# Cosine and sine rows of the inverse feature transform on two 64-row lanes of TensorE, with a new order

## Chip, cores and metric

One core of one Trainium2 chip runs the whole kernel. The time is device microseconds of one execution; the median of the runs counts. Engines are named as in the profile: PE (TensorE matmul) and PEld (its weight loads), DVE (VectorE), ACT (ScalarE), POOL (GpSimd) and SP (the queue that issues most DMAs).

## What is computed

Two mixers of the same x (2048 rows, 640 features) are blended row by row with a gate.

```python
def _A_ref(x, wqkv, wo):            # 32 heads of 20, 8 keys back at a distance of 2
    qkv = (x @ wqkv) ...
    logits = jnp.einsum("bhsd,bhswd->bhsw", q, kg) * scale
    attn = _softmax(jnp.where(mask, logits, -1e9), axis=-1)
    o = jnp.einsum("bhsw,bhswd->bhsd", attn, vg)
    return o.reshape(B, S, D) @ wo
def _B_ref(x, w_r, w_i):            # spectral filter
    X = jnp.fft.rfft2(x, axes=(-2, -1)) * (w_r + 1j * w_i)
    return jnp.fft.irfft2(X, s=(S, D), axes=(-2, -1))
g = _sigmoid((x * gate_w).sum(-1, keepdims=True))
return g * _A_ref(x, wqkv, wo) + (1 - g) * _B_ref(x, w_r, w_i)
```

## The kernel before

The 2048 rows are 16 p + j, with p on the 128 partitions and j = 0 to 15. `qkv` multiplies x with the projection (fp32 split into two fp32r parts, three products each) and stores the result to DRAM. `attend(par, h)` does four heads for the even or the odd j: DVE multiplies and reduces, POOL does the products with v (tiles pv), ACT copies, masks and the exponential. Its results (tiles o) go to DRAM (`od`) in pieces of two or four j, and `project_even`/`project_odd` read them back (`ot`), transpose them on PE (`oTp`) and multiply with wo (`woa`, `wob`).

The spectral branch folds x and transforms it over blocks of rows (`cols`, into `zg`), then sixteen groups g of frequencies run through `freq(g)`: the transform over features (u, v, ab), the rest of the row transform (x, z), the filter (P, wp), the two combinations s = P + z and P - z, and matmuls (tile `g`) that put rows of frequencies of the features onto the partitions of `zg`. Group 0 is the exception: two tables `back` instead of one, of which only some chunks of 128 need both.

`spatial(j)` is the inverse transform over features. Per j, six fp32 matmuls read `zg[:, t, j]` (t = 0 to 4, 128 feature frequencies each) as weights and `gt` (cosine and sine tables) as moving data, into two PSUM banks: `oa` gets the cosine rows and `ob` the sine rows, for even frequencies in the first 161 columns and odd ones in the next 161. The 128-row chunks straddle the four blocks of frequencies, so three of the chunks (1, 2 and 3) carry parts of two blocks, with zeros beside them. ACT copies both banks into `os`; four matmuls with `fct` (`ha`, `hb`) do the last step over rows, and ACT and DVE combine these with the attention's part into the output.

`work` records the operations in a natural order; `ORDER`, a table of numbers, then says in which order they are issued, and each engine runs its own in that order. All operations are issued through one line of the recorder (L386 before, L400 after), so tiles and not lines tell them apart. Each fp32 matmul shows as two MATMUL records in the trace. Buffers are rings of named places: `osr` (places for os), `ps(banks, name)` (PSUM banks). While the last heads of the attention are at work on DVE and POOL, PE runs `spatial` and the even projections; the odd projections are last, since they need the last heads.

Of the kernel before, what the change touches and what calls it, by code (L numbers as in the profile page):

```python
# [26 lines left out]

BP = (0, 1, 2, 3, 4, 5, 6)
# [3 lines left out]
def dft_tables():  # L32
# [7 lines left out]
    ke, ko = PERM[:161], PERM[161:]  # L40
    kb = PERM[2:161]
# [86 lines left out]
    def ck(k):  # L128
        return (np.where((k == 0) | (k == 320), 1.0, 2.0) / (S * D))[:, None]

    gt = np.zeros((640, 644))
    gt[0:161, 0:161] = np.cos(tau * np.outer(ke, d) / D) * ck(ke)
    gt[161:321, 161:322] = np.cos(tau * np.outer(ko, d) / D) * ck(ko) * (d < 160)
    gt[321:480, 322:483] = -np.sin(tau * np.outer(kb, d) / D) * ck(kb) * ((d > 0) & (d < 160))
    gt[480:640, 483:644] = -np.sin(tau * np.outer(ko, d) / D) * ck(ko) * (d > 0)
    gt = np.concatenate(
        [gt[0:128, 0:161], gt[128:256, 0:322], gt[256:384, 161:483], gt[384:512, 322:644], gt[512:640, 483:644]], 1
    )
# [15 lines left out]
class Engine:  # L154
# [50 lines left out]
{Wp48S^xk5{}S0j0stWa8~^|S5YJf5;2e()-dz9y0sAKZbW)=m>G~>ja#c?We=xxAfB@%${{m#x=b59`IdyTU{vq(yT@9sNe+BS{#HY+m)y=f!_RR8qRRBGA*}EW<uG2O+6A~}&R!D}&rV+x2jv1iJ  # L205
<-;gAir31;1Wf;>N>_o7_jkA<(T8Z}8f9+iVn*m~XGw&Dh4Q!g^!a-g;gRa_JDi6k#N9Iq<cZ2&JtcN76xX8*H9m++$L@A2#7kr>_z#tF%`KR?`)4zIcgHuNs+E`A0h0RujinI`1a|acnWK|Ere?@m
HR<GJdrLg8yDWOSIr*!MnId|XGp+qg;T23}HTJ=%(|W2(cSJH>)~(8ZXW6h>)0cUw(=(QERf0KOldi#P1i?WzT;Se6a||?lQgj~UmUG5v9Vn$>Bc}N8Iu)~M<1Wb(flHSj=Mu8b)c65D0UPTFIc$Q0
(eX9!O&5nj_$BX_(~F9Vbf!8Ozo0}fas_15zX7wEL;UuN2DXv*gTgLLBUH$^XgrP86i()d5+t3$VQRVU&`?%f)J^gaQkrt4YRK(uDSz6ys_<TP+v5B;kH9QqeHgo&uN?m5AydT{pLVlVOz{PO#Ijb6
+O)yXvOe&%NTw*a$ST7*T<`qoAH_gB75y1xXe|0>)lG%X*=7)4y&BU8^%*Xm6kh^Sg@lD{shw^{Z>fEm_IWhUF=K})%fC!6Fu70lFWo4rl)ap!;kHt`wJM?oKvv5;@mVMtBuwKD*4XhlYDu64#9kT{
LoY#86kzka)pPYf{N*4lfK|Z`J#<q`QZ_NaBFw(H%5Gx%$;!^X72{O@^sJrZv7k2nT2?{L0+;ot9F2h=*pz$=f&9oS(6R^=ve{df4Gv?SdS^LyH{tD9&i%;LlvR{wM*}SdvKKhASw?r!2at5#wz1@l  # L210
9qY$vBtM<%u&tdpjfO8Q;LOjzBL@R(X;g~)IPHm!_!rfJWL2THq&fzt!SDG>NLd6jG8dsdP1x#@MTG1W8uupzQlqVf<?Zn~FIA5l;+ETlX)e1Gvzk5Y(@KkltoII>Oq!}M<Uj%<$xl-i02$*HCS++k
zm7E!#<`$Z7Yt8Gk2*^Z@BvF>GQYM8Z*-TV?Kv0@qJF7f##CZ{y(YlGre6%8HrPr~ixycNU8D>G-?9=}{k$zQ7)`hKh3T2u(N}Khye~H#4Zu%~nt-$nP)gB+g_bvw;6!_2OJ1ZwNXWd+nivju$$Yw@
{h9EDLO`#cu0#7Fl%mr0w&ZwEG%_6<h{D)%uq5*G?j(=S$tlo1;dHxkC&sxr)AOMS7V~kRCl%$unp=pl>QB*_Gkdbs20DC$hI>tUiHYX@CRY0MrbuB|+IvRMnL`gm{`hUMh%=gs^!hX4hbW9<5mmSS
XEZ~;h~u_dmXo?8Ks6l!JlFu20k?{6q8m94^*#as=7R1ctF`$$B^`Ail-%HNAtoEC6QKtbyka-BLg;E<!xU!~^($8uvMN@^Y6q(}W%9@W9-)~@TzYtEg+@=5Z(Armx<=7lYZ?!>1G0&GS`i<jmKyP$
HmAy)ivl`kmitYwTKoN!Zj7@-A9p~Dpa((OWe??q%4t9K)exM$udFC_`SXg83|Ght1}1^%!o<snP@qnI*)XkJmJZ$d&YCSfYQ4?xSj$-`Xj5|lAR5Cuj9bI7u?u_BJd9=ihe<!VQVHaV^|bX~r-)1P
V|6MIih|dFGNQ4M`jqCg>Zn`!UA*cd)B3p;hV+tVJ3rxZOy2XSUYfTXSuav(Q*5M5P#?>UbaW1ZRvv_k#dt>44!0Qsa`V_FAqZ%H^GIWd<`o{JgMj3{Wx+e7*dmOf$J_K*J5{bxl(gOepgchq0O`!T
# [40 lines left out]
class Mixer:  # L257
# [17 lines left out]
    def places(self, pp, dr, sb):  # L275
# [15 lines left out]
        def ring(*tags):  # L291
            return Ring(sb, *tags)
# [24 lines left out]
    def ps(self, banks, name):  # L317
        if banks not in self.banks:
            self.banks[banks] = Ring(self.pp, *(f"bank{i}" for i in banks))
# [648 lines left out]
```

## Time and profile before

| what | value |
|---|---|
| median of 3 runs | 448.94 us (448.38 to 449.37) |
| profiled execution | 449.34 us, its span 447.5 us |
| PE busy | 438.6 us, 98% of the span |
| DVE busy | 408.7 us, 91% |
| POOL busy | 362.4 us, 81% |
| ACT busy | 211.2 us, 47% |
| DMA | 110.75 MB, 247 GB/s |

Groups of instructions are given as: engine, operation, out<-in by the program's names without numbers, shape, count, then busy time, mean duration of one in ns, and the engine's idle time before them with its cause. Chain rows give start, length and what ran; an "x8" counts records. In windows each engine's busy time stands in the order PE, PEld, DVE, ACT, POOL, followed by the granted clock of PE and the share and rate of DMA.

### The profile page before, as it was taken

Reading aid. Unit: us, or ns where it says so; the run is one execution under the profiler, and the core shown is the slowest. Engines: PE = TensorE matmul, PEld = TensorE weight load, DVE = VectorE, ACT = ScalarE, POOL = GpSimd, SP = SyncE. Lnnn points to the kernel's source line nnn. Section 1 sums busy time; section 2 is a strip of 40 time slices with the busy share of each in tenths; the row PEclk is TensorE's granted clock in tenths of the full one; section 3 lists DMA queues with packets and bytes.
Section 4 is the critical chain, followed back from the end, with each engine's and each line's share of the span. In section 5 each row is a group of like instructions: output and inputs, shape, how many; then the busy total and the mean of one; then the engine's idle time right before and its main releaser. Section 6 shows DMA issues by size and latency. Waiting matters only on the chain.

```text
span 447.5 us, 7258 instructions
## 1 busy us (share of the span) xinstructions
PE 438.6 (98%) x2440; PEld 390.1 (87%) x2440; DVE 408.7 (91%) x519; ACT 211.2 (47%) x561; POOL 362.4 (81%) x316
## 2 busy tenths in 40 slices
PE   9999999999999999999998999999999999999996
PEld 6888888888889889898887779998978999999996
DVE  4989989999999999999999999999999997899575
ACT  5443155363344634245548666677554564352110
POOL 1237984999999999997998999858899998899900
PEclk9999999999999999999999999999999999999999
DMA  8999999879489969789979789979976131366642
GB/s 325 390 349 321 313 325 369 299 205 312 131 240 325 341 181 325 204 279 313 319 219 311 235 274 297 313 218 308 295 200 204 31 99 42 96 218 228 184 177 88
DMA packets 73957, 110.75 MB, mean 247 GB/s; under 512 B 21297, under 2 KB 50993, under 8 KB 73921
## 3 DMA queue, kind: packets, MB, share of 16 engines
q1 hardware_dynamic: 40192, 69.32, 47.7%
q10 hardware_dynamic: 32816, 36.97, 26.7%
q0 software_dynamic: 912, 4.00, 2.3%
q8 instruction: 19, 0.31, 0.3%
q14 instruction: 18, 0.14, 0.1%
HBM read 72.51 MB, written 32.84 MB: 235 GB/s over the span
## 4 chain that ended last, share of the span: by engine, by line
PE 92%; DMA 2%; DVE 1%; ACT 1%; POOL 1%; issue 1%; ACTq 0%; POOLq 0%; DVEq 0%
PE qkv L386 47%; PE woa L386 8%; PE wob L386 7%; PE z L386 5%; PE ob L386 4%; PE oa L386 4%; PE g L386 4%; PE u L386 3%; PE v L386 2%; PE oTp L386 2%; PE ha L386 2%; PE x L386 2%; PE hb L386 2%; DMA P<-X 1%; DMA ot<-od 1%
## 5 line engine op out<-in xcount | busy, mean ns | idle before, releaser
L386 PE MATMUL qkv<-w,xo 128*128 128x480 f32 (+1 forms) x480 | 117.2, 388 | 0.0
L386 PE MATMUL qkv<-w,xe 128*128 128x480 f32 (+1 forms) x474 | 106.8, 382 | 0.0
L386 PEld LDWEIGHTS qkv<-w,xe 128*128 128x128 f32 x474 | 89.5, 189 | 14.8 <-ACT w L386 0.5
L386 PEld LDWEIGHTS qkv<-w,xo 128*128 128x128 f32 x480 | 88.4, 189 | 12.2
L386 ACT COPY ev<-qkv 128x480 f32<-128x480 f32 x64 | 35.1, 560 | 60.5 <-PE qkv L386 50.3
L386 PE MATMUL woa<-wo,oT 128*128 128x320 f32 x240 | 51.3, 330 | 0.2 <-DVE oT L386 0.2
L386 PE MATMUL wob<-wo,oT 128*128 128x320 f32 x240 | 49.5, 323 | 0.0
L386 POOL TENSOR_TENSOR P<-P,wp 128x963 f32<-128x963 f32 (+1 forms) x16 | 35.4, 2210 | 7.3 <-DMA P<-X 7.3
L386 PEld LDWEIGHTS woa<-wo,oT 128*128 128x128 f32 x240 | 38.2, 189 | 1.4 <-DVE oT L386 0.6
L386 PEld LDWEIGHTS wob<-wo,oT 128*128 128x128 f32 x240 | 37.7, 189 | 0.5 <-ACT ya L386 0.2
L386 POOL TENSOR_TENSOR fx<-fx 128x158 f32<-128x158 f32 (+1 forms) x16 | 11.7, 748 | 25.0 <-DVE fx L386 18.5
L386 POOL TENSOR_TENSOR w<-raw,w 128x480 fp32r<-128x480 f32 (+1 forms) x20 | 25.2, 1275 | 6.6 <-ACT w L386 6.5
L386 ACT CAST oT<-oTp 128x384 fp32r<-128x384 f32 (+1 forms) x32 | 13.2, 427 | 33.7 <-PE wob L386 13.2
L386 PEld LDWEIGHTS g<-mm,s 128*128 128x128 f32 x150 | 21.7, 190 | 6.0 <-ACT zg L386 4.0
L386 PE MATMUL g<-mm,s 128*128 128x128 f32 x150 | 24.9, 281 | 1.5 <-ACT zg L386 1.5
L386 PE MATMUL ob<-gt,zg 128*128 128x161 f32 (+1 forms) x96 | 22.7, 345 | 0.0
L386 PE MATMUL oa<-gt,zg 128*128 128x161 f32 (+1 forms) x96 | 22.6, 345 | 0.0
L386 PE MATMUL v<-bt,zc 128*128 128x240 f32 (+2 forms) x96 | 21.2, 327 | 1.1 <-ACT zc L386 1.1
L386 PE MATMUL u<-bt,zc 128*128 128x240 f32 (+2 forms) x96 | 20.8, 323 | 0.4 <-DVE ab L386 0.4
L386 DVE TENSOR_TENSOR oT<-oTp,oT 128x384 fp32r<-128x384 f32 (+1 forms) x32 | 15.1, 484 | 4.8 <-ACT oT L386 4.4
L386 PEld LDWEIGHTS v<-bt,zc 128*128 128x128 f32 x96 | 16.0, 190 | 4.0 <-ACT zc L386 1.4
L386 ACT CAST w<-raw 128x480 fp32r<-128x480 f32 (+1 forms) x30 | 17.0, 593 | 4.9 <-DMA raw<-in_wqkv 2.1
(304 smaller groups left out, 1120.0 us busy)
## 6 DMA issues: line engine op xcount, KB each, us to landing
qkvd<-ev ACTq DMA_DIRECT2D x32, 480.0 KB, 5.3
wp<-in_ws SPq DMA_DIRECT2D x16, 642.0 KB, 5.4
raw<-in_wqkv SPq DMA_DIRECT2D x25, 240.0 KB, 5.9
fx<-in_x SPq DMA_DIRECT2D x8, 641.0 KB, 7.5
ot<-od SPq DMA_DIRECT2D x16, 320.0 KB, 4.2
P<-X ACTq DMA_DIRECT2D x30, 160.5 KB, 4.7
fd<-fx POOLq DMA_DIRECT2D x6, 640.0 KB, 5.9
f<-fd SPq DMA_DIRECT2D x6, 640.0 KB, 5.6
```

The costliest lines, as they stand in the source:

```text
L386: p.dve.memset(w, 0.0)
```

## The change

`gt` is laid out anew. Frequencies 1 to 320 of the features go in five strips of 64, and a strip's cosine rows lie on partitions 0 to 63 (lane 0), its sine rows on partitions 64 to 127 (lane 1). `freq` writes s in that form: strip t has 64 sums and 64 differences side by side as one 128-column weight. The sine of frequency 320 is zero, and its place in lane 1 takes the constant term, which is therefore the first column of `ob` and is added to the even cosine part as the bias of an ACTIVATE. In `spatial`, ten matmuls of 64 rows take the place of six of 128: for each strip one from lane 0 into `oa` and one from lane 1 into `ob`, recorded as one operation by the new `Engine.run`, so that nothing comes between them. The program gives lane 0 the upper half of the array (position 0, size 64x128) and lane 1 the lower half (position 64).

Group 0 now uses both tables for all five strips (ten matmuls instead of six). ACT's two copies to `os` become three operations, and one ACTIVATE of one column for each group writes the constant term. `oa` and `ob` take turns through four banks instead of three, `ha` has bank 4 alone for odd j and banks 4 and 7 for even j, and `os` has five places instead of three. The tables that follow from this are smaller (`gt` 968 columns for 1288).

```diff
+STRIPS = (
+    (2, (0, 322), (0, 323)),
+    (0, (0, 161), (0, 162)),
+    (1, (0, 161), (1, 161)),
+    (3, (161, 161), (162, 161)),
+    (4, (161, 161), (162, 161)),
+)
...
+    gt, c = np.zeros((128, 968)), 0
+    for t, *parts in STRIPS:
+        for lane, (a, n) in enumerate(parts):
+            gt[64 * lane : 64 * lane + 64, c : c + n] = lanes[lane, 64 * t : 64 * t + 64, a : a + n]
+        c += n
...
+    def run(self, name, parts):
+
+        def all_of(parts):
+            for a, k in parts:
+                getattr(self.real, name)(*a, **k)
+
+        self.plan.record(self.eng, "run", all_of, (parts,), {})
...
 ORDER = """
-{Wp48S^xk5{}S0j0stWa8~^|S5YJf5;2e()-dz9y0sAKZbW)=m>G~>ja#c?We=xxAfB@%${{m#x=b59`IdyTU{vq(yT@9sNe+BS{#HY+m)y=f!_RR8qRRBGA*}EW<uG2O+6A~}&R!D}&rV+x2jv1iJ
+{Wp48S^xk5{}S0j0stWa8~^|S5YJf5;2b*)YFz*T0sAKZbW)=m>G~>ja#c?We=xxAfB@%${{m#x=b59`IdyTU{vq(yT@9sNe+BS{#HY+m)y=f!_RR8qRRBGA*}EW<uG2O+6A~}&R!D}&rV+x2jv1iJ
...
-        self.osr, self.hor, self.hyr, self.yer = n("raw", 3), n("x", 4), ring("x4", "x5"), ring("x6")
+        self.osr, self.hor, self.hyr, self.yer = ring("raw0", "raw1", "raw2", "ev0", "ev1"), n("x", 4), ring("x4", "x5"), ring("x6")
...
-        s = self.s12r.next(f"s{g}", 768)
-        d0 = 321
+        s = self.s12r.next(f"s{g}", 10 if g == 0 else 5, 2, 64)
+        sums = s[:, 0:5, 0], s[:, 5:10, 1] if g == 0 else s[:, :, 1]
+        pz = [a.rearrange("p (t r) -> p t r", t=5) for a in (P[:, 0, 1:321], z[:, 1:321])]
+        V.tensor_add(sums[0], *pz)
+        V.tensor_sub(sums[1], *pz)
         if g == 0:
-            d0 = 449
-            G.memset(s[:, 384:449], 0.0)
-        V.tensor_add(s[:, 0:321], P[:, 0], z)
-        V.tensor_sub(s[:, d0 : d0 + 319], P[:, 0, 2:], z[:, 2:])
+            G.memset(s[:, 0:5, 1], 0.0)
+            G.memset(s[:, 5:10, 0], 0.0)
+            G.memset(s[:, 5, 1, 0:1], 0.0)
+        A.activation(out=s[:, 0, 1, 0:1], in_=z[:, 0:1], func=AF.Identity, bias=P[:, 0, 0:1])
...
-                for w, back in chunks[t0 + i]:
+                for back in range(2 if g == 0 else 1):
...
-        o1, o2 = (self.ps((0, 1, 2), f"o{i}{j}") for i in "ab")
-
-        def mm(o, t, r, start, stop):
-            T.matmul(o, zg[:, t, j], r, start=start, stop=stop, skip_group_check=True)
-
-        mm(o1[:, 0:322], 1, gt[:, 161:483], True, False)
-        mm(o1[:, 0:161], 0, gt[:, 0:161], False, False)
-        mm(o1[:, 161:322], 2, gt[:, 483:644], False, True)
-        mm(o2[:, 0:322], 3, gt[:, 805:1127], True, False)
-        mm(o2[:, 0:161], 2, gt[:, 644:805], False, False)
-        mm(o2[:, 161:322], 4, gt[:, 1127:1288], False, True)
-        os = self.osr.next(f"os{j}", 644)
-        oq = os.rearrange("p (b a d) -> p a b d", b=2, a=2)
-        A.copy(oq[:, 0], o1[:, 0:322].rearrange("p (b d) -> p b d", b=2))
-        A.copy(oq[:, 1], o2[:, 0:322].rearrange("p (b d) -> p b d", b=2))
+        o1, o2 = (self.ps((0, 1, 2, 3), f"o{i}{j}") for i in "ab")
+        parts, c = [], 0
+        for t, *halves in STRIPS:
+            for i, (o, (a, n)) in enumerate(zip((o1, o2), halves)):
+                part = o[:, a : a + n], zg[64 * i : 64 * i + 64, t, j], gt[64 * i : 64 * i + 64, c : c + n]
+                parts.append((part, dict(start=(t == 2), stop=(t == 4), skip_group_check=True)))
+            c += n
+        T.run("matmul", parts)
+        os = self.osr.next(f"os{j}", 645)
+        A.copy(os[:, 322:645], o2[:, 0:323])
+        A.activation(out=os[:, 0:161], in_=o1[:, 0:161], func=AF.Identity, bias=os[:, 322:323])
+        A.copy(os[:, 161:322], o1[:, 161:322])
         yield
-        h1, h2 = self.ps((3, 4), f"ha{j}"), self.ps((5,), f"hb{j}")
+        h1, h2 = self.ps((4,) if j % 2 else (4, 7), f"ha{j}"), self.ps((5,), f"hb{j}")
```

The order changes from its 382nd operation on. On PE, at the first `oa` of the kernel, the six matmuls of an index stood among those of its neighbours and among `hb` and the transposes (the number behind a name is j, or the group for g; the number after the underscore is the buffer's):

```order
L386 MATMUL oTp0_860<-ident_69,ot12_858 128x128 x3
L386 MATMUL g15_3_815<-mm13_771,s15_813 128x128 x2
L386 MATMUL oa3_878<-gt_327,zg_211 128x322
L386 MATMUL oa1_872<-gt_327,zg_211 128x322
L386 MATMUL oa1_872<-gt_327,zg_211 128x161 x2
L386 MATMUL ob1_873<-gt_327,zg_211 128x322
L386 MATMUL ob1_873<-gt_327,zg_211 128x161
L386 MATMUL oa3_878<-gt_327,zg_211 128x161
L386 MATMUL ob1_873<-gt_327,zg_211 128x161
L386 MATMUL ob3_879<-gt_327,zg_211 128x322
L386 MATMUL hb1_876<-os1_874,fct_71 128x161
```

Now the same place on PE begins a stretch of lanes alone (L177 is the line in `Engine.run`):

```order
L400 MATMUL g15_3_815<-mm13_771,s15_813 128x128 x2
L400 MATMUL oTp0_860<-ident_69,ot12_858 128x128 x3
L177 MATMUL oa1_872<-gt_327,zg_211 128x322
L177 MATMUL ob1_873<-gt_327,zg_211 128x323
L177 MATMUL oa1_872<-gt_327,zg_211 128x161
L177 MATMUL ob1_873<-gt_327,zg_211 128x162
L177 MATMUL oa1_872<-gt_327,zg_211 128x161
L177 MATMUL ob1_873<-gt_327,zg_211 128x161
```

Lanes 0 and 1 alternate, and four indices (1, 3, 5, 7) follow one another, 40 matmuls, before PE comes to `oTp`, `ha` and `hb` again. In all the 160 matmuls on lanes stand in five such stretches, of 40, 30, 50, 30 and 10.

On ACT, just behind the same place, the banks were emptied in this order (vt4a is a load that ACT issues, qbank, L5b and ya belong to the attention):

```order
L386 COPY qbank_63<-q4b_576 128x160
L386 COPY os1_874<-oa1_872 128x2x161
L386 DMA vt4a_565<-qkvd_64 128x1200
L386 COPY os1_874<-ob1_873 128x2x161
L386 COPY os3_880<-oa3_878 128x2x161
L386 COPY qbank_63<-q4b_576 128x160
L386 ACTIVATE ho1_877<-hb1_876,ng_74 128x322
L386 COPY os3_880<-ob3_879 128x2x161
L386 COPY os5_885<-oa5_883 128x2x161
```

And now, for j = 3, 5 and 7 (L4a is a mask that ACT writes into the logits of the head, after DVE has made them):

```order
L400 COPY os3_880<-ob3_879 128x323
L400 ACTIVATE os3_880<-oa3_878,os3_880 128x161
L400 COPY os5_885<-ob5_884 128x323
L400 COPY os7_891<-ob7_890 128x323
L400 DMA q4b_576<-qkvd_64 128x640
L400 COPY L4a_567<-low_80 1x16x4
L400 ACTIVATE os5_885<-oa5_883,os5_885 128x161
L400 COPY os5_885<-oa5_883 128x161
L400 ACTIVATE L5b_551<-L5b_551 128x256
L400 ACTIVATE os7_891<-oa7_889,os7_891 128x161
L400 COPY os7_891<-oa7_889 128x161
```

The `oa` of j = 5 is emptied behind the mask L4a, and that of j = 7 behind L5b's exponential.

On DVE, around the last reduce of the attention (o4b6, for j = 13 and 15), the order was:

```order
L386 TENSOR_REDUCE o4a6_596<-pv4a6_597 128x160
L386 TENSOR_TENSOR y12_974<-ha12_967,h12_969 128x321
L386 SCALAR_TENSOR_TENSOR y1_981<-woa1_992,g_73,y1_981 128x320
L386 TENSOR_TENSOR oT5_997<-oTp0_998,oT5_997 128x384
L386 TENSOR_TENSOR oT5_997<-oTp3_999,oT5_997 128x256
L386 TENSOR_REDUCE o4b6_598<-pv4b6_599 128x160
L386 SCALAR_TENSOR_TENSOR y1_981<-wob1_993,g_73,y1_981 128x320
```

And it is now:

```order
L400 SCALAR_TENSOR_TENSOR y1_981<-wob1_993,g_73,y1_981 128x320
L400 SCALAR_TENSOR_TENSOR ha14_975<-ha14_975,ng_74,h14_977 128x161
L400 TENSOR_TENSOR y14_979<-ha14_975,h14_977 128x321
L400 TENSOR_TENSOR oT5_997<-oTp3_999,oT5_997 128x256
L400 TENSOR_REDUCE o4a6_596<-pv4a6_597 128x160
L400 SCALAR_TENSOR_TENSOR y3_987<-woa3_1000,g_73,y3_987 128x320
L400 TENSOR_TENSOR oT7_1005<-oTp0_1006,oT7_1005 128x384
L400 TENSOR_TENSOR oT7_1005<-oTp3_1007,oT7_1005 128x256
L400 TENSOR_REDUCE o4b6_598<-pv4b6_599 128x160
```

The reduce comes behind the outputs of j = 1 and the combination of j = 14, ahead of which it stood: 477th of DVE's 519 instructions, where it was 474th.

More of the change, by code (lines that the diff above doesn't have):

```diff
@@ L129, in ck @@
         return (np.where((k == 0) | (k == 320), 1.0, 2.0) / (S * D))[:, None]
[L131 to L138, printed above, removed]
+    lanes = np.zeros((2, 320, 323))
+    for at, a, k, fits in ((0, 0, PERM[1:161], (d > 0) & (d < 160)), (160, 161, ko, d > 0)):
+        fitc = (d < 160) | (at == 0)
+        lanes[0, at : at + 160, a : a + 161] = np.cos(tau * np.outer(k, d) / D) * ck(k) * fitc
+        lanes[1, at : at + 160, a + 1 : a + 162] = -np.sin(tau * np.outer(k, d) / D) * ck(k) * fits
+    lanes[1, 0] = 0
+    lanes[1, 0, 0] = 1 / (S * D)
+    gt, c = np.zeros((128, 968)), 0
[3 more added lines that the diff above has]
+        c += n
     f = np.float32
@@ new lines @@
+FIo&uC=rTCG^332n*e4@1I8_Pp|;?Q1QFGcxB-#|GS~LA(^EhN(DVpb`MU*=byh=F*yquh`Iq5#d?5nVCXAf*aAFNz{Y_VOzYE1HXf2WN=7dJ8-xDM>9wt;XARM*?l4cr!x?wJ$fC;lQ#AlkYSvttQ
+LM14tn$Xj8dih9p`Md<VH3fwii9;yN3D{BfoQ2BOOCobu3f?3aoqk01r})J1v31zZR6FVz01KW(1seb{62BuarlL@`TR^#5!v~X-tU0lgN;FNTbB7-zXGIgwrPHqE`|b%YiVpC!dn4Y$HCrdNb^~MX
+W91!D6jWZz=Oa^brZ$52Jia{hMhXY&<<|XoPsh720at07sl>gjKc;!?W>h^%YIg==w>ikaHeHOXNwc^PvdRa&204?la^gJ02+m4WedriBbSM6{x?xhMEl#w&hxyJoZ@E7caE_`7Rqvg?SGR>G0&`UZ
+u!k6(t*%hG@uMZF@3N8en`!BUcc77%so%U}uc-zH=-Ttr)%a|AvUfY$gA#kEwguZzem@WkB9GQ~qb=0<3Q$ym204zmA<bHJRa&VBWq@7+>b5=5^P_EO7{{@5&rgNEL`&-zT2%?04i2eJmfsA^ZrTm*
@@ L236 @@
+??F>fX_^NI<G5n+MgCe4u+1FXcTLFiPK-*-@1Sq@L=T{l182WS+Oxj#uuSg{fI(h!=ZeSZwm<`)>5FR?WShdG9839FRJIn1L_=AM@N(se=&hn2tB88b;iE<#$}VZFq((Q)8~YVvIs~+jLJd3k1I^ig
+e!Vj#k`-!U!L?8Ec{a#98LT5<5pd1T<I-RrilniF3~47HcQ1`iO1<O;g1m*{1_;S#Jy-{rb|4l(8c7UFl^~}jU}pt--wC&3>=)and8<&7T#&>10000000I6Oyf^>={WXEXr~nH50ssI2003E9
 """
@@ L318, in ps @@
         if banks not in self.banks:
-            self.banks[banks] = Ring(self.pp, *(f"bank{i}" for i in banks))
+            self.banks[banks] = Ring(self.pp, *(f"bank{i}" if i < 7 else "qbank" for i in banks))
         return self.banks[banks].next(name, 512)
@@ L355, in work @@
         S.dma_start(self.sign, ins["t_sign"])
-        self.bt, self.gt = self.one("bt", 1288, tag="e0"), self.one("gt", 1288, tag="e1")
-        S.dma_start(self.bt[:, 0:1122], ins["t_bt"])
+        self.bt, self.gt = self.one("bt", 1122, tag="e0"), self.one("gt", 968, tag="e1")
+        S.dma_start(self.bt, ins["t_bt"])
         S.dma_start(self.gt, ins["t_gt"])
@@ L730, in freq @@
             for i in range(n):
-                for w, back in chunks[t0 + i]:
+                for back in range(2 if g == 0 else 1):
                     m = tb[:, 1024 + 128 * back : 1152 + 128 * back] if g == 0 else tb[:, 192:320]
                     T.matmul(
-                        o[0 : w.shape[1], i * 128 : i * 128 + 128],
-                        w,
+                        o[:, i * 128 : i * 128 + 128],
+                        s[:, t0 + i + 5 * back].rearrange("p b r -> p (b r)"),
                         m,
-                        start=(i == 0),
+                        start=(i == 0 and back == 0),
                         stop=(i == n - 1),
```

57 lines of the change are left out of this document (21 added, 36 removed).

## Prediction

> **What bounds the kernel now.** I read the page first, then the order of the critical chain, then the stage from 341.5 us on, because that is where the inverse feature transform (tiles oa and ob) runs.
>
> ```profile
> span 447.5 us, 7258 instructions
> PE 438.6 (98%) x2440; PEld 390.1 (87%) x2440; DVE 408.7 (91%) x519; ACT 211.2 (47%) x561; POOL 362.4 (81%) x316
> PE 92%; DMA 2%; DVE 1%; ACT 1%; POOL 1%; issue 1%; ACTq 0%; POOLq 0%; DVEq 0%
> 341.50:402.90 61.40, 61.40 (x384) 55.91 (x382) 56.15 (x77) 29.66 (x79) 56.32 (x46) 1.00 0.35 106
> 402.90:447.50 44.60, 40.55 (x285) 40.03 (x284) 30.73 (x68) 6.57 (x16) 20.97 (x25) 1.00 0.51 169
> ```
>
> The last two rows are windows: length, then busy time of PE, PEld, DVE, ACT, POOL. PE is on 92% of the chain that ends last and has no gap at all from 341.5 to 402.9 us, at a granted clock of 1.00. What PE stops doing there comes off the end, as long as nobody else sets the end. DVE and POOL are the ones to fear: each is busy 56 of those 61.4 us with the last heads of the attention. After 402.9 us both have room, and PE runs the eight odd projections.
>
> The profiled execution took 449.34 us, 1.84 more than its span; the median shown is 448.94, 0.4 lower. I make the sum on 449.34 and take off 0.4 at the end. About 0.2% (0.9 us) is what a measurement of this kernel can tell from no change, since its three runs lie within 0.99 us.
>
> **The inverse transform on PE.** The rows give the price of a column.
>
> ```profile
> 341.55 1.63 PE oa L386 x8
> 345.36 0.82 PE oa L386 x4
> 252.89 0.45 PE g L386 x4
> 305.22 0.67 PE g L386 x6
> ```
>
> An fp32 matmul shows as two MATMUL records, so the x8 of the first row are two of 322 columns and two of 161: 966 columns in 1.63 us, 1.69 ns each. The second row, 483 columns in 0.82 us, says 1.70. Before, an index j takes 322+161+161 twice, 1288 columns, 2.17 us, and sixteen take 34.8 us. The change makes ten matmuls of 64 rows out of these six of 128: five for oa with weights on partitions 0 to 63 (966 columns) and five for ob on 64 to 127 (968 columns). No row of before shows a matmul on 64 rows. If the two halves of the array stream side by side, j costs 967 columns, 1.63 us, and sixteen 26.1 us: **-8.7 us**. If they take turns, j costs 1934 columns, 3.27 us, and sixteen 52.3 us: +17.5 us. I take side by side: the halves have their own rows, their own partitions of zg and gt and, in oa and ob, different banks, and the parts are issued alternately, so that each record of one half has one of the other to go with it.
>
> The Trainium skill says of such tiles ("TensorE: Matmul & The Clock Gate", Part 3, on packing small matmuls) that matmuls of different row groups run at once, and it has 3.07 times the speed for four of 32 rows. At that share of the ideal, 77%, an index would cost an estimated 2.1 us, and hardly anything of the 8.7 would be left; no run here shows either.
>
> Around it PE gets more work. Feature group 0 had six matmuls into its g banks and now has ten, because every chunk needs both tables: four more of 128 columns, at 0.45/2 us each by the x4 row above, **+0.9 us**. Within a block of consecutive lanes the ob half trails by one record (161 columns at half of 1.69 ns, 0.136 us). The order has five such blocks (40, 30, 50, 30 and 10 matmuls), **+0.7 us**.
>
> At both ends of a block PE goes over between 128-row and 64-row work, ten times.
>
> ```profile
> L386 PEld LDWEIGHTS oa<-gt,zg 128*128 128x128 f32 x96 | 15.9, 190 | 1.9
> L386 PE MATMUL oa<-gt,zg 128*128 128x161 f32 x64 | 13.0, 300 | 0.0
> L386 PEld LDWEIGHTS oTp<-ident,ot 128*128 128x128 f32 x80 | 10.7, 140 | 1.6 <-DVE oT L386 0.7 <-DMA ot<-od 0.5
> ```
>
> A record of 161 columns lasts 300 ns, though by the price of a column the next one starts 136 ns after it. If an array must be empty before its shape changes, a change costs the difference, 0.16 us; if the weights can only be loaded then, another 0.19 us; at the least it costs nothing. Ten changes lie between 0 and 3.5 us; I take the middle reading, **+1.6 us**, which is nearest to what the MATMUL row shows by itself. The Trainium skill states the drain ("TensorEngine Tiling (Array Packing)", Tiling Modes): going to another tiling mode drains the engine. By that rule alone the sum would hold the 1.6 us, without it 0; no row of before has such a change in it.
>
> **ACT.** It empties the banks, and its two copies for an index become a copy of 323, an ACTIVATE of 161 that adds the constant term as a bias, and a copy of 161.
>
> ```profile
> L386 ACT COPY os<-oa 128x322 f32<-128x322 f32 x16 | 6.9, 429 | 10.4 <-PE oa L386 10.4
> L386 ACT COPY os<-ob 128x322 f32<-128x322 f32 x16 | 6.8, 427 | 7.9 <-PE ob L386 7.8
> L386 ACT COPY z<-qkv 128x1 f32<-128x1 f32 x16 | 2.4, 164 | 5.8 <-PE qkv L386 5.5 <-ACT L7b L386 0.3
> L386 ACT COPY qbank<-q5a 128x160 f32<-128x160 f32 x4 | 1.2, 303 | 0.0
> PEld hb L386 <- ACT os L386: 0.2, 1, 0.2
> ```
>
> That is 0.43+0.30+0.30 = 1.03 against 0.86 us, 2.7 us over sixteen, and 16 new ACTIVATEs of one column (0.16 each, 2.6 us) ahead of the g matmuls. ACT waits 18 us for oa and ob in those rows, and it is busy 29.7 of 61.4 us there, so I put both at nothing. The cover is thin in one place: j=5 and j=9 want the banks that j=1 and j=5 leave, and in the new order ACT has a mask copy that waits for DVE and POOL (L4a) ahead of emptying oa5. Four banks instead of three give PE one index, 1.6 us, of grace. Without the cover each block can lose about a copy chain, 1 us: 0 to 3 us, and 0 taken, since the last row, a wait, is the only one of before in which PE waits for os: 0.2 us in all.
>
> **DVE, POOL and DMA.** DVE's two rows for s go from 321 and 319 to 320 and 320 columns: nothing. Three memsets of group 0 on POOL and the smaller table (968 for 1288 columns) touch nobody. The reordering does. On DVE the s of group 15, which PE needs before the first oa, stands three instructions further on (the 375th and 376th of 519, where they were the 372nd and 373rd).
>
> ```profile
> 300.00:341.50 41.50, 40.18 (x261) 35.66 (x260) 40.07 (x61) 24.47 (x66) 38.31 (x28) 1.00 0.84 252
> 404.76 0.41 PE L386 MATMUL woa<-wo,oT 128*128 128x320 f32 x1
> 413.73 1.48 DVE L386 TENSOR_REDUCE o4b<-pv4b 128x160 f32<-128x1280 f32 x1
> 415.13 0.54 DVE L386 SCALAR_TENSOR_TENSOR y<-wob,g,y 128x320 f32<-128x320 f32 x1
> 416.70 4.62 SPq L386 DMA_DIRECT2D ot<-od  x2
> 431.49 0.56 DVE L386 TENSOR_TENSOR oT<-oTp,oT 128x384 fp32r<-128x384 f32 x1
> DMA to landing us min/median/max: 1.7/2.5/4.0
> ot<-od SPq DMA_DIRECT2D x16, 320.0 KB, 4.2
> ```
>
> Up to 341.5 us DVE has 1.4 us to spare. Three instructions are worth 1.6 us at the 0.54 of a small row, quoted below it, and up to 4.4 if all were reduces of 1.48. Set against the 1.4 us of slack, the first oa starts 0 to 3 us later; I take **+1.0 us**, nearer to the small rows.
>
> The last reduce of the attention (o4b, 413.73 to 415.2 us) also stands three instructions further on (477th for 474th), 1.6 us. Behind it hang the store to od, the load of ot for j=13 (second of the two in the SP row, issued by 421.3) and its transposes, which DVE finishes from 431.5 us on. From 415.2 to 431.5 are 16.3 us. The store (2.5, the row of landings, which is o4b's) and the load (4.2) take 6.7 of them. Some 10 us are free, so 1.6 later and an end 5 us sooner still fit: nothing.
>
> **Sum:** 449.34 - 8.7 + 0.9 + 0.7 + 1.6 + 1.0 = 444.8; less 0.4, **444.4 us**. With the favourable bounds (no drain, no late start, no offset) it is 441.1; with the unfavourable ones (3.5, 3.0 and ACT's 3.0) 451.3.
>
> **Rivals.**
>
> *The weights are the limit (slower).* An index now loads 20 times instead of 12, each time 128 columns. In the g row of 305.22 a record with its load goes by in 0.112 us, the shortest interval of fp32 weights here, so a load takes no longer; the transposes' loads are 50 ns shorter than the others (140 and 190 ns). Two loads must go by in each 136 ns. If loads of the two halves pass one after the other at 0.112, j costs 2.24 us, sixteen 35.8: +1.0 in place of -8.7. With the other terms 449.34+1.0+0.9+1.6+1.0 less 0.4 is 453.4 us. From 0.068 us a load this begins to eat the gain, at about 0.1 it has eaten it. For it: PEld is busy 87% already. Against: two halves can take their weights at once if they can take their data at once. The Trainium skill puts a load at columns over 1.2 GHz whatever the rows ("TensorE: Matmul & The Clock Gate", LDWEIGHTS). By it a load of 64 rows would cost as much as one of 128, an estimated 107 ns, and the g row agrees with 112.
>
> *The halves take turns.* +17.5 in place of -8.7 and no offset: 449.34+17.5+0.9+1.6+1.0-0.4 = 469.9 us. For it: nothing in the trace shows an overlap. Against: the separate partitions and banks.
>
> *The gain is there and the attention takes it.* DVE and POOL are over 91% busy from 341.5 to 402.9; if the last o4b comes over 4 us later than 416.8, the 10 us are used up with PE's 5, and every us more is paid at the end: 448 to 449.5. For it: POOL's last pv4b rows, which feed that reduce, also stand later in the order. Against: DVE has 14 us free after 402.9.
>
> **Chances.** Side by side with the small costs: 0.68. Attention takes it: 0.07, half of it within 0.2% and half faster. Weights: 0.13. Taking turns: 0.12. So faster 0.715, same 0.035, slower 0.25, in round numbers 0.71, 0.04 and 0.25. The range goes from 440, a little under the favourable sum since the reordering may also close gaps of PE's last 44.6 us (4 are idle), to 453.5, with the weights inside. Outside are taking turns (0.12) and some 0.06 below 440.
>
> **What would show it.** Right: oa and ob at about 1.63 us for an index in the chain, ob records starting within one of oa's; PE's busy time down by about 7; the first woa of j=1 near 399 us instead of 404.8; no waits of PE for ACT os. A chain in which oa and ob come to 2.2 us for an index means weights, 3.3 means turns. Gaps of 0.2 to 0.4 us around the blocks are the drain. If PE is idle before j=13 and waits for ot, the attention has taken it. The forecast is wrong if the time is over 448.

## The result

| | before | after |
|---|---|---|
| median | 449.91 us (18 runs, 448.38 to 455.91) | 455.45 us (18 runs, 452.15 to 459.41) |
| ratio, 95% interval | | 1.0112 [1.0089, 1.0135] |
| profiled execution, its span | 449.34, 447.5 us | 453.08, 451.0 us |
| first record of oa | 341.4 us | 350.6 us |

The change makes the kernel 1.1% slower; 444.4 us was forecast, with a range up to 453.5. Executions come at a granted clock near 1.00 or near 0.995, the latter mostly 2 to 4 us longer and in a share that differs from run to run (15 of the 18 of after), so the experiments have a second median, of the fast executions at a clock of 0.998 or more (453.63 for after, 448.8 to 449.9 for before on the chips of the experiments), and the profiles below are of that kind unless a clock is given.

**The lanes do what was forecast.** The page of after, then PE's timeline at the last index, then the critical chain from the first index on (start, length, what ran):

```profile
span 451.0 us, 7548 instructions
PE 435.0 (96%) x2576; PEld 384.9 (85%) x2576; DVE 409.1 (91%) x519; ACT 214.9 (48%) x593; POOL 363.2 (81%) x318
```

```profile
403.55 0.30 PE L177 MATMUL oa<-gt,zg 64*128 64x161 f32 x1
403.57 0.30 PE L177 MATMUL ob<-gt,zg 64*128 64x161 f32 x1
403.69 0.29 PE L177 MATMUL oa<-gt,zg 64*128 64x161 f32 x1
403.71 0.29 PE L177 MATMUL ob<-gt,zg 64*128 64x161 f32 x1
...
408.25 0.41 PE L400 MATMUL wob<-wo,oT 128*128 128x320 f32 x1
```

```profile
350.31 0.39 PE oTp L400 x3
350.70 0.47 PE oa L177
...
352.55 0.26 PE oa L177
...
354.20 0.25 PE oa L177
...
355.85 0.24 PE oa L177
...
357.50 0.26 PE oTp L400
```

A record of ob starts 0.02 us after one of oa, and the next pair 0.14 us later, which is the 0.136 us of 161 columns. An index follows the other after 1.65 us (352.55, 354.20, 355.85). Four indices with both ends take 357.50 - 350.70 = 6.80 us, where 4 x 1.63 is 6.52: this block's ends cost 0.28 us. By the same chain the five blocks take 6.80, 5.14, 8.49, 5.15 and 1.85 us, 27.4 in all. From the first oa to the first matmul of the odd projections are 408.25 - 350.63 = 57.6 us; before they were 404.76 - 341.4 = 63.4. That is **5.7 us less** (5.75 by unrounded starts). Behind that point both kernels need 42.7 us to the end of the span.

**The loss lies ahead of the first oa.** Windows of after up to the first oa and behind it (length, then PE, PEld, DVE, ACT, POOL, the granted clock, DMA):

```profile
300.00:350.60 50.60, 47.78 (x309) 42.31 (x307) 45.43 (x71) 31.47 (x88) 44.59 (x33) 1.00 0.73 212
350.60:405.50 54.90, 54.49 (x506) 50.16 (x505) 51.13 (x73) 32.19 (x96) 49.66 (x42) 1.00 0.49 150
```

In before DVE was busy 40.07 of 41.50 us there; now it is 45.43 of 50.60, so it has 5.2 us of idle time where it had 1.4. The first oa comes 9.2 us later, and 9.2 - 5.7 = 3.5 is the difference of the spans. Who waits for whom between 240 us and the first oa, of before and then of after (sum, times, longest):

```profile
POOL P L386 <- DMA P<-X: 7.3, 5, 2.8
DVE z L386 <- POOL P L386: 1.0, 2, 0.5
```

```profile
ACT s L400 <- DVE s L400: 13.9, 11, 3.1
POOL P L400 <- DMA P<-X: 11.3, 5, 4.0
DVE z L400 <- POOL P L400: 6.8, 5, 3.0
PEld z L400 <- ACT s L400: 1.8, 5, 0.9
PEld iz L400 <- ACT s L400: 1.7, 1, 1.7
```

The first row is new. `ACT s` is the one-column ACTIVATE that writes the constant term; the rows below it are the loop of a group: PE makes x and z, ACT makes X, a DMA exchanges X's halves into P (P<-X), POOL multiplies, DVE combines z and makes s. ACT's timeline at group 5:

```profile
285.81 0.26 ACT L400 ACTIVATE s<-z,P 128x1 f32<-128x1 f32 x1 [2.85 <-DVE s L400]
285.97 0.19 ACT L400 COPY L6b<-low 1x16 f32<-1x16 f32 x1
286.10 0.43 ACT L400 COPY P<-x 128x321 f32<-128x321 f32 x1
286.42 0.52 ACT L400 COPY zc<-zg 128x384 f32<-128x384 f32 x1
```

ACT stands 2.85 us for a column of 0.26 us, with P, zc and X of later groups queued behind it.

### The profile page after: what moved, and what is told of

The parts are those of the page before. It is cut to its first block, busy times and chain, and to the rows that moved or that the text cites. A ratio compares the mean times of both kernels' runs of the same rounds, so it can differ in the third digit from the quotient of the medians.

```text
span 451.0 us, 7548 instructions
## 1 busy us (share of the span) xinstructions
PE 435.0 (96%) x2576; PEld 384.9 (85%) x2576; DVE 409.1 (91%) x519; ACT 214.9 (48%) x593; POOL 363.2 (81%) x318
## 3 DMA queue, kind: packets, MB, share of 16 engines
q10 hardware_dynamic: 32816, 36.97, 27.4%
## 5 line engine op out<-in xcount | busy, mean ns | idle before, releaser
L400 ACT COPY ev<-qkv 128x480 f32<-128x480 f32 x64 | 34.8, 560 | 56.4 <-PE qkv L400 47.2
L400 PE MATMUL wob<-wo,oT 128*128 128x320 f32 x240 | 50.8, 327 | 0.0
L177 PE MATMUL ob<-gt,zg 64*128 64x161 f32 (+2 forms) x160 | 27.7, 327 | 0.0
L177 PE MATMUL oa<-gt,zg 64*128 64x161 f32 (+1 forms) x160 | 27.6, 327 | 0.0
L177 PEld LDWEIGHTS oa<-gt,zg 64*128 64x128 f32 x160 | 23.7, 186 | 3.1 <-issue 0.7
L177 PEld LDWEIGHTS ob<-gt,zg 64*128 64x128 f32 x160 | 23.8, 186 | 0.0
```

Of the source, the lines that this page charges most:

```text
L177: getattr(self.real, name)(*a, **k)
L400: p.dve.memset(w, 0.0)
```

## The experiments

Theory 1: ACT's sixteen ACTIVATEs hold up the loop. It came to have two forms: 1a, by what is queued behind them on ACT; 1b, by the time for which z's PSUM bank and P's place wait for their last reader. Theory 2: the new order of the groups costs the 9 us by itself. Later a theory 1c came in, on the exchange's DMA. "Order of before" is short for: the order of before for everything up to the first oa, that of after from there on. Ratios are to before, run beside it on the same chip; "second median" is the fourth column.

| run | what | median us | at a clock of 0.998 or more: median us (executions) | ratio, 95% interval | first oa us (profile) |
|---|---|---|---|---|---|
| | after | 455.45 | 453.63 (3) | 1.0112 [1.0089, 1.0135] | 350.6 |
| e1 | after, term by DVE, in ACT's old place | 463.25 | none | 1.0226 [1.0131, 1.0320] | 364.0 (clock 0.985) |
| e2 | after, no term | 448.42 | 448.00 (8) | 0.9950 [0.9909, 0.9991] | 345.2 |
| e3 | order of before, ACTIVATE as late as it can be | 454.89 | 452.70 (5) | 1.0089 [1.0041, 1.0137] | 349.6 |
| e4 | before, plus an ACTIVATE that reads z and P | 455.44 | 452.35 (4) | 1.0065 [1.0017, 1.0113] | 344.8 |
| e5 | after, term by DVE, right behind s | 451.59 | 450.67 (6) | 1.0032 [1.0001, 1.0062] | 348.2 |
| e6 | order of before, term by DVE, right behind s | 448.20 | 448.13 (10) | 0.9974 [0.9940, 1.0008] | 344.9 |
| e7 | order of before, no term | 448.50 | 447.34 (8) | 0.9966 [0.9931, 1.0001] | 348.4 (clock 0.996) |
| e8 | after, lanes in turn | 468.72 | 468.72 (2) | 1.0399 [1.0343, 1.0454] | 352.6 (clock 0.996) |
| e9 | after, ACTIVATE reads s, not z and P | 448.71 | 448.71 (12) | 0.9959 [0.9933, 0.9985] | 347.7 (clock 0.998) |
| e10 | e7 with six matmuls in group 0 | 446.02 | 446.01 (5) | 0.9904 [0.9876, 0.9932] | 415.2 (clock 0.755) |
| e11 | before, four matmuls of group 0 twice | 450.92 | 450.53 (8) | 1.0038 [1.0006, 1.0070] | 343.1 |
| e12 | before, plus an ACTIVATE that reads s | 450.70 | 450.48 (8) | 1.0016 [0.9979, 1.0052] | 343.5 |
| e13 | after, term copied from beside s | 454.03 | 452.50 (4) | 1.0081 [1.0045, 1.0116] | 353.3 (clock 0.996) |
| e14 | order of before, term copied from beside s | 449.77 | 448.22 (8) | 0.9994 [0.9951, 1.0038] | 346.1 |
| e15 | before, exchanges 3 and 5 delayed | 451.02 | 450.93 (9) | 1.0010 [0.9974, 1.0046] | 345.6 (clock 0.996) |
| e16 | before, exchanges 6 and 7 delayed | 450.57 | 450.46 (10) | 1.0007 [0.9970, 1.0045] | 344.5 |
| e17 | after, two loads of wp later | 452.30 | 452.09 (9) | 1.0029 [0.9996, 1.0063] | 350.2 |
| e18 | order of before, ACTIVATE right behind s | 449.67 | 449.31 (10) | 0.9999 [0.9964, 1.0034] | 344.7 |

### Is it the ACTIVATE? (e1, e2, e3, e4)

```diff
 e1   -A.activation(out=s[:, 0, 1, 0:1], in_=z[:, 0:1], func=AF.Identity, bias=P[:, 0, 0:1])
 e1   +V.tensor_add(s[:, 0, 1, 0:1], P[:, 0, 0:1], z[:, 0:1])
 e2   -A.activation(out=s[:, 0, 1, 0:1], ...)
 e4    V.tensor_sub(s[:, d0 : d0 + 319], P[:, 0, 2:], z[:, 2:])
 e4   +A.activation(out=s[:, d0 + 318 : d0 + 319], in_=z[:, 320:321], func=AF.Identity, bias=P[:, 0, 320:321], scale=-1.0)
```

e3 changes the table of numbers alone.

> The kernel after, its order untouched, but the constant term of each group is written by a one-column add of DVE in the place of ACT's one-column ACTIVATE. Before is 449.9 us, after 455.5 (medians of 18 runs each). Theory 1 (ACT's ACTIVATE waits for DVE's s and holds up what is queued behind it on ACT, and z's bank and P's place with it): most of the 9 us that the first oa came late are won back, 446 to 449 us, first oa of the profiled run at 342 to 345 us instead of 350.7. Theory 2 (the new order of the feature-frequency stage costs the 9 us, whoever writes the constant term): 454 to 457 us, first oa still near 350.

> The kernel after, its order untouched, with the constant term left out altogether (frequency 0 of the features is missing from the result), so that neither ACT nor DVE has the sixteen instructions. Theory 1: 445 to 448 us, at most 2 us below the version with DVE's sixteen adds (16 adds of some 0.1 us). Theory 2: 454 to 457 us.

> The kernel after with the order of before for everything up to the first oa (the group-0 extras and ACT's one-column ACTIVATE put in, the latter as late as z's bank and P's place allow), and the order of after from there on. Theory 1: ACT's ACTIVATE is still there, so most of the loss stays: 450 to 456 us. Theory 2: the order of before brings the first oa back to 342 to 343 us and the whole to 443.5 to 446 us.

> The kernel before, with one more instruction in each group: right behind DVE's subtraction for s, ACT writes the last column of s once more with the same value (a one-column ACTIVATE of z and P that waits for DVE's subtraction). Nothing else is changed, the order is that of before. Theory 1: slower than before by 4 to 9 us, 454 to 459. Theory 2: at most 1 us slower, 449.5 to 451.

Without the term (e2) 7.0 of the 455.45 us are gone, 5.6 by the second median and 5.5 between the profiled executions (453.08 and 447.60), and the first oa stands at 345.2. With the order of before but the ACTIVATE still there (e3) 454.89 us remain: theory 2 falls. Alone on the kernel before (e4) the ACTIVATE makes it slower by 0.65%, 0.2 to 1.1%. The first oa is 3.4 us late there, as is the second median against that of before beside it (452.35 and 448.99), less than the 4 to 9 that theory 1 gave.

e1 went against every expectation: on DVE the term costs more than on ACT. Its waits between 240 and 351 us show why:

```profile
DVE z L400 <- POOL P L400: 11.0, 5, 4.8
ACT P L400 <- DVE s L400: 7.6, 4, 4.6
PEld iz L400 <- DVE s L400: 4.5, 1, 4.5
```

The add stood in the ACTIVATE's place of the order, behind DVE's operations for s and in several groups behind long ones of the attention on DVE (a reduce of 1.48 us at 264.27, between the subtraction and the add at 265.67). Until then nobody may write the next z into its bank (the third row) nor the next P into its place (the second). That made theory 1b.

### How long z and P are held (e5, e6, e7, e9)

e5 and e6 move the add directly behind the subtraction. e7 has no term. e9 keeps the ACTIVATE and its place and changes what it reads:

```diff
 e9   -A.activation(out=s[:, 0, 1, 0:1], in_=z[:, 0:1], func=AF.Identity, bias=P[:, 0, 0:1])
 e9   +A.activation(out=s[:, 0, 1, 0:1], in_=s[:, 0, 1, 1:2], func=AF.Identity)
```

> As the version with DVE's one-column add, but that add stands directly behind the subtraction on DVE, where in the first attempt up to 4.6 us of other work stood between the two and z's bank and P's place stayed taken so long. Everything else in the order of after. Theory 1 (what costs is how long the last reader of z and P is kept waiting, on whatever engine): close to the version without the term, 16 adds of 0.1 us more, 448 to 451 us. Theory 2a (DVE has no room for sixteen more instructions, each of them holding up the attention): 455 us or more, as in the first attempt.

> DVE's one-column add directly behind the subtraction, and the order of before for everything up to the first oa, of after from there on. Theory 1 with the order as the rest of the loss (the version without the term still began its first oa 3.7 us later than before): 444 to 447 us, first oa at 342 to 343.5. If the order costs nothing and the rest is something else (group 0's four extra matmuls, noise): 448 to 451, first oa at 345 or later.

> The constant term left out altogether (frequency 0 of the features is missing from the result), with the order of before up to the first oa and of after from there on. If the order costs 3 to 4 us: 443 to 445.5 us, first oa at 341.5 to 343. If it costs nothing: 447.5 to 449, as in the order of after, first oa at 345.

> The kernel after, its order untouched, but ACT's one-column ACTIVATE reads a value of s that DVE's subtraction wrote, in place of z and P (the constant term is wrong by that). ACT still waits for DVE at the same place of its queue, and PE's g matmuls still wait for ACT, but z's bank and P's place are free as soon as DVE has read them. If the harm is what is queued behind the waiting ACTIVATE on ACT: 454 to 457 us, as after. If the harm is the longer hold on z's bank and P's place: 448 to 450 us, as without the term. In between: both, in that proportion.

The same sixteen adds take the kernel to 1.0226 of before in the late place and to 1.0032 in the early one: 8.7 us for the place alone. (The medians, 463.25 and 451.59, are 11.7 us apart, but e1 has no second one.) e7 and e2, 448.50 and 448.42, differ in the order only; by the second median, each against before beside it, the order is worth 1.0 us there, and with the add on DVE 2.5 (e5 to e6). e9 comes out at 448.71, as if there were no term, though ACT waits as often as in after and not much shorter (13.9 us there):

```profile
ACT s L400 <- DVE s L400: 10.3, 11, 2.4
```

So in this run a waiting ACTIVATE with a queue behind it does not cost the time, which speaks against theory 1a; e13, below, speaks for it.

### The same on before, and with the right result (e12, e13, e14, e18)

```diff
 e12  +A.activation(out=e, in_=e, func=AF.Identity)      # e = s[:, d0 + 318 : d0 + 319]
 e13  -V.tensor_add(sums[0], *pz)                        # five times 64 columns
 e13  +V.tensor_add(s[:, 0:5, 0:65], ...)                # five times 65, from one column earlier; s is 129 wide for a strip
 e13  +A.activation(out=s[:, 0, 65:66], in_=s[:, 0, 0:1], func=AF.Identity)
```

e14 is e13 with the order of before. e18 is the kernel after with the order of before and the ACTIVATE right behind the subtraction.

> The kernel before with sixteen one-column ACTIVATEs of ACT as in the earlier run on before, right behind DVE's subtraction, but each copies the last column of s onto itself, so that it waits for DVE in the same place of ACT's queue and reads neither z nor P. Theory 1b (the hold on z's bank and P's place): no more than 1 us slower than before, 449.5 to 451. Theory 1a (what stands behind the waiting ACTIVATE): as the run that read z and P, 453 to 456 us.

> The kernel after with the constant term right and without the hold: DVE's sum for s takes 65 columns for each strip instead of 64, the first of them the column before the strip, so that column 0 lands beside s, and ACT copies it from there into its place; nothing on ACT reads z or P any more. Order of after (in group 10 the copy goes behind the sum). Theory 1b: as the run in which ACT read a value of s, 447.5 to 449.5 us. Theory 1a: 454 to 457.

> The same, with the order of before for everything up to the first oa (the copy right behind DVE's subtraction) and of after from there on. Theory 1b, with the order worth 1 to 2.5 us as between the runs without the term and those with DVE's add: 446 to 448 us, under both kernels. Theory 1a: 452 to 456, as the run with this order and ACT reading z and P.

> The order of before up to the first oa and of after from there on, ACT's ACTIVATE of z and P as in the kernel after, but right behind DVE's subtraction in the order, not as late as possible. It differs from the run with the copy from beside s in this order (449.8) only in what ACT reads and in DVE's five columns, and from the run with the ACTIVATE as late as possible (454.9) only in its place. Theory 1b (the hold on z's bank and P's place): 2 us or more over the copy from beside s, 451.5 to 454. If the late place alone made that run slow: 449 to 451.

e12 and e4 differ only in what ACT reads: 450.70 against 455.44 us (1.9 us apart by the second median), in the direction of theory 1b, but the intervals of the ratios overlap. The clean pair is e3 and e18, with the same instructions, reading z and P, and only the place of the sixteen changed: 454.89 late, 449.67 early (3.4 us apart by the second median), with intervals that don't meet. Their waits between 240 and 351 us, e3 and then e18:

```profile
PEld z L401 <- ACT s L401: 6.2, 10, 0.8
PEld g L401 <- ACT s L401: 4.1, 5, 1.5
```

```profile
PEld z L401 <- ACT s L401: 2.4, 4, 0.9
PEld g L401 <- ACT s L401: 2.7, 4, 1.5
```

In e3 PE waits ten times for ACT before it may write the next z. But e18 falls short of its expectation of 451.5: held only briefly, z and P cost at most about 1 us against the copy from beside s (e14, 449.77; 1.1 us by the second median). The length of the hold fits the pair; but the place in ACT's queue changes with it, and the pair doesn't separate the two.

e13 does not fit theory 1b: nothing on ACT holds z or P there, and yet it takes 454.03 us in the order of after, in the range of theory 1a, where e9 takes 448.71. e14, at 449.77, lies between the ranges of the two.

### The exchange against the loads of wp (e15, e16, e17)

The traces of e13 and after have something in common that e9 lacks: some exchanges take long. Taken from the rows of the issues and of POOL's products, an exchange of group 3 took 4.4 to 5.6 us from its second DMA to POOL's product in all runs that issued it 0.3 us or more ahead of a 642 KB load of weights wp on the other queue, and 6.1 to 7.6 in all that issued it less than 0.2 ahead or behind, e13 and after among them; e4 alone has a long one (6.5) with a lead, of 0.5. Theory 1c: that race is the cause.

```diff
 e15  +A.copy(dly, bt[:, 0:321]); A.copy(dly, bt[:, 321:642])     # groups 3 and 5; e16: 6 and 7
       A.dma_start(P[0:64, 1:3], X[64:128])
 e17  +S.dma_start(wp[0:1, 0, 0:1], ins["ws"][g][0:1, 0, 0:1])     # groups 6 and 9
       S.dma_start(wp, ins["ws"][g])
```

> The kernel before, with two ACT copies of 321 columns into an unused place (0.9 us of ACT together, waiting for nothing) ahead of the exchange's DMAs of groups 3 and 5, and nothing else changed. In the profile of before these two exchanges are issued 0.92 and 0.72 us ahead of the 642 KB load of weights wp on the other queue; the delay takes that lead away. Theory 1c (an exchange issued with or behind the wp load lands 1.5 to 3 us later, as in the groups where the profile of after loses): the two exchanges take 6.5 to 7.5 us from issue to POOL's product where they took 5.5 and 4.7, and the time is 3 to 6 us longer than before, 452.5 to 456. Without the race: twice 0.9 us at the most, 449.5 to 451.5.

> The same two copies ahead of the exchanges of groups 6 and 7, which in the profile of before are issued 2.33 and 1.55 us ahead of the wp load, so that a lead of 0.6 to 1.4 us is left. Theory 1c: no exchange takes longer than before by over 0.5 us, and the time is 0 to 2 us longer than before, 449.5 to 451.5, clearly less than with groups 3 and 5. If any delay of an exchange costs the same: as the run with groups 3 and 5.

> The kernel after with ACT's ACTIVATE as it is, but the wp loads of groups 6 and 9 wait on their queue for a DMA of one element into the same place (about 2 us), so that the exchanges of groups 5 and 8, which were issued 0.47 us behind and 0.02 us ahead of those loads, are now ahead by 1.5 us or more. Theory 1c: these exchanges take 5 us in place of 7.7 and 6.3, and the time is 2 to 5 us under that of after, 450.5 to 453.5. If the loads are not what holds the exchange up: 454.5 to 457.

Group 5 in after (ACT's queue, SP's queue, POOL) and in e17:

```profile
272.25 0.61 ACTq L400 DMA_DIRECT2D P<-X  x1
...
271.78 0.33 SPq L400 DMA_DIRECT2D wp<-in_ws  x1
...
279.96 2.23 POOL L400 TENSOR_TENSOR P<-P,wp 128x963 f32<-128x963 f32 x1 [5.27 <-ACT zg L400]
```

```profile
272.31 0.61 ACTq L400 DMA_DIRECT2D P<-X  x1
...
273.09 0.35 SPq L670 DMA_DIRECT2D wp<-in_ws  x1
...
275.68 2.24 POOL L400 TENSOR_TENSOR P<-P,wp 128x963 f32<-128x963 f32 x1 [0.93 <-DMA P<-X]
```

With the load 0.8 us behind the exchange instead of 0.5 ahead, POOL begins 3.4 us after the issue instead of 7.7. The exchange is held up by the load, or by what SP issues right behind it (kt5b and ot, which moved with it), and the row's own releaser (ACT zg) is not what ended that wait: in e17 the same zg runs at 279.55, behind the product. Of the 4.3 us the first oa keeps 0.4 (350.2 for 350.6), since the exchanges of groups 6 and 7 now take 7.2 and 7.5; the median falls by 3.1, the second one by 1.5. On before the race was hardly brought about: in e15 the lead of group 3 went from 0.92 to 0.07 us and its exchange from 5.5 to 6.1, group 5's load moved along with its exchange, and the time is that of the control e16. Its 451.02 us lie in the range given for no race, but with one exchange 0.6 us longer that doesn't decide.

The traces of after and e2, which differ in the ACTIVATEs alone, show more. Group 3 in after and in e2:

```profile
252.09 0.48 ACTq L400 DMA_DIRECT2D P<-X  x1
252.10 0.33 SPq L400 DMA_DIRECT2D wp<-in_ws  x1
258.59 2.22 POOL L400 TENSOR_TENSOR P<-P,wp 128x963 f32<-128x963 f32 x1 [4.03 <-DMA P<-X]
```

```profile
251.83 0.48 ACTq L400 DMA_DIRECT2D P<-X  x1
252.22 0.33 SPq L400 DMA_DIRECT2D wp<-in_ws  x1
256.29 2.23 POOL L400 TENSOR_TENSOR P<-P,wp 128x963 f32<-128x963 f32 x1 [1.60 <-DMA P<-X]
```

The exchange is issued 0.26 us later, level with the load instead of 0.39 ahead of it, and POOL begins 2.3 us later. The exchanges of groups 3, 5 and 8 take 6.5, 7.7 and 6.3 us in after where those of e2 take 4.5, 5.9 and 5.1: 5.1 us together, nearly the 5.4 by which the first oa differs; the other groups' differences nearly cancel. They are issued 0.01 us ahead, 0.47 behind and 0.02 ahead of the load, in e2 0.39 ahead, 0.31 behind and 0.55 ahead. So that is where the ACTIVATEs' loss lies in these two traces; that the race alone makes it is not shown, since e17 gained only 0.4 of the 4.3 us. **Open:** why e13 loses 5.3 us to e9 (3.8 by the second median). Its exchanges of groups 3, 5 and 8 take 7.1, 7.4 and 7.7 us where those of e9 take 5.1, 6.4 and 6.9; that is 3.8 us if all of it lies on the path, and no run moved these three alone.

### Lanes in turn, and group 0 (e8, e10, e11)

```diff
 e8   -T.run("matmul", parts)
 e8   +T.run("matmul", parts[0::2] + parts[1::2])
 e10  -for back in range(2 if g == 0 else 1):
 e10  +for back in ((0,), (0,), (0, 1), (1,), (1,))[t0 + i] if g == 0 else (0,):
 e11  +T.matmul(out, w, m, start=False, **go)            # once more, for the four of group 0 with one table
```

> The kernel after with the ten matmuls of an index issued in another order: the five of lane 0, then the five of lane 1, and nothing else changed. If the gain of the lanes comes from a record of one having one of the other beside it: an index takes 3.2 to 3.3 us in the chain instead of 1.64, sixteen 26 us more, 478 to 483 us. If neighbouring records of one lane could also run side by side, or the lanes were not the reason for 1.64: no change, 453 to 458.

> The version without the constant term and with the order of before up to the first oa, and with six matmuls in group 0 instead of ten, as before had them (frequency 0 of the features is missing, and a part of the first group of row frequencies). If group 0's four extra matmuls are what still keeps the first oa late: 0.5 to 1.5 us below the version with ten (448.5 median), 447 to 448. If they are hidden: no difference.

> The kernel before with four of group 0's six g matmuls done twice (that group's part of the result is wrong by it), nothing else changed. If the four cost what the prediction put on them, 0.9 us, and nothing hides them: 0.5 to 1.5 us slower than before. If PE has that much room in front of the first oa: no difference.

e8's chain:

```profile
352.63 1.42 PE oa L177 x7
354.06 0.14 PE ob L177
354.19 0.14 PE oa L177
354.33 0.93 PE ob L177 x6
...
355.54 0.93 PE oa L177 x6
...
356.74 0.93 PE ob L177 x6
```

An index now takes 2.41 us (354.33 to 356.74), 0.76 more than side by side, 12.2 for sixteen; the median rose by 13.3. It is neither 1.65 nor the 3.27 that I expected of turns: the first record of the other lane starts while three of this one are still to come (ob at 353.77, oa's last three from 353.90 on), so the ends of two runs overlap.

Group 0: four matmuls more on before make the first oa 1.7 us late (343.1) and the time 0.38% longer, 0.06 to 0.70%, that is 1.7 us, 0.3 to 3.1; four fewer (e10 against e7) save 2.5 us of median. By the second median the two are 1.1 and 1.3 us, within the 0.5 to 1.5 of the expectations.

## Why the prediction was wrong

**The step that failed** is the one headed ACT: "16 new ACTIVATEs of one column (0.16 each, 2.6 us) ahead of the g matmuls [...] so I put both at nothing". It set their busy time against ACT's idle time behind 341.5 us, while all sixteen lie ahead of the first oa, in the stage where I had seen 1.4 us of room on DVE, and it asked neither what they read nor what stands behind them. Each waits for DVE (13.9 us in all in after). It is the last reader of z's bank and of P's place, and ACT's copies and the DMAs of the exchange are queued behind it. Worth, by e2: 5.4 us of the first oa, 5.6 of the second median, 7.0 of the first. One of the ACTIVATEs takes 0.26 us, not 0.16, which matters little. That I weighed the instruction against its own engine's idle time, and not against who waits behind it and who needs its operands back, is the error.

That the ACTIVATEs cost the time is shown by e2. Which way they cost it is settled only in part. In the traces nearly all of it lies in three exchanges that are issued 0.2 to 0.5 us later against the loads of wp than without the term. What makes them late is open in the order of after: e9, which frees z and P early, wins all but 0.7 us of it back by the second median, while e13, which frees them too, wins back 1.1.

**Term by term.**

- Lanes, -8.7: right. 1.65 us an index where I had 1.63.
- Offset and drains, +0.7 and +1.6 for five blocks: together the blocks take 27.4 us, 1.3 more than sixteen times 1.63, where I had 2.3; oversized, and in the right place.
- With these three the stage should have shrunk by 6.4 us and did by 5.7. That they are so close is luck: the blocks take 7.4 us less than the 34.8 of before, and the rest of PE's work in the stage takes 1.7 us more, for which I had no term. PE's wait in it, below, has its like in before (0.42 us for oT at 403.35), and what else there is was not traced.

```profile
405.69 0.81 PE L400 MATMUL hb<-os,fct 128*128 128x161 f32 x4 [0.45 <-ACT h L400]
```

- Group 0, +0.9: 1.7 in e11, with 0.3 to 3.1, and 1.1 by the second median; right as far as the runs can tell.
- First oa later by +1.0 (0 to 3): it came 9.2 later. Of these, 5.4 are the ACTIVATEs (e2) and some 1.7 group 0 (e11), for which I had a term of its own. The remaining 2.1 (345.2 - 341.4 - 1.7) are within my bounds, but not settled: with no term the two orders differ by 1.0 us in the second median and by nothing in the first.
- Last o4b, hidden: right; both kernels need 42.7 us from the first odd projection to the end.

The sum by these: 449.34 - 5.7 + 9.2 + 0.2 (what lies around the span grew from 1.84 to 2.08) = 453.0, and the profiled execution took 453.08.

**Rivals.** Weights as the limit (453.4) gives nearly the profiled time by the wrong way: an index does not take 2.24 us, and the loads of a pair start as close together as its matmuls.

```profile
350.63 0.18 PEld L177 LDWEIGHTS oa<-gt,zg 64*128 64x128 f32 x1 [0.17 <-issue]
350.64 0.18 PEld L177 LDWEIGHTS ob<-gt,zg 64*128 64x128 f32 x1
350.74 0.19 PEld L177 LDWEIGHTS oa<-gt,zg 64*128 64x128 f32 x1
350.75 0.19 PEld L177 LDWEIGHTS ob<-gt,zg 64*128 64x128 f32 x1
```

Turns (469.9) did not occur; e8 had to force them. The attention takes nothing behind 402.9. The drain, that the Trainium skill states ("TensorEngine Tiling (Array Packing)", Tiling Modes), agrees with what is seen: the first load of the block waits 0.17 us. The Trainium skill's 3.07 for four tiles ("TensorE: Matmul & The Clock Gate", Part 3) does not carry over to two of 64 rows: 3.27 us of columns in 1.65 us is 1.98 times.

The forecast named what would show it wrong, a time over 448. Of its five right signs three came: the index, the pairs, and no waits of PE for os beyond the 0.2 us of before. The first woa near 399 us is where the loss appeared (408.5). And PE's busy time fell by 3.6 us (438.6 to 435.0), not 7: by itself a record of 161 columns counts 0.30 us, in a stream 0.14, and where PE waits in the stage ahead more of them stand by themselves. That reading fits the 433.8 us of e2, but was only argued.

## What to carry to other kernels

Cost a small new instruction by its operands and by what its engine issues behind it, not by its length: find the place that its input leaves (a PSUM bank, a ring's buffer), who writes there next, and how far behind the previous reader the new one is issued; the same sixteen adds cost 8.7 us more in the late place than in the early one. A DMA that it makes 0.26 us late can lose 2.3 us, as group 3's did, where a large load starts beside it. Where a loop goes over several engines and a DMA, idle time of one engine in the next stage is no cover for it. And compare with the version without the thing at once: leaving out the constant term told in one run what the order's many differences hid.

## What was not expected of the hardware

- Two fp32 lanes of 64 rows run side by side, weight loads included: 1.98 times, and 160 loads for each lane of 186 ns in the median, with starts 0.01 us apart.
- With lanes in turn PE still overlaps the ends: the other lane starts three records early, 2.41 us an index.
- An exchange of two 160 KB DMAs on ACT's queue took 7.7 us up to POOL's product with a 642 KB load 0.5 us ahead of it on SP's queue, and 3.4 us with that load, and the two that SP issues behind it, 0.8 us or more behind it.
- The best of these versions with the right result (e6) is 1.4% under after by the ratios and not measurably under before: 0.9974 [0.9940, 1.0008].
